# Rebuilding float64 weights in a borrowed PSUM buffer, with three smaller changes, in a fused RWKV-6 scan and feed-forward kernel

## The chip, the cores and the metric

The kernel runs on one core of one Trainium2 chip. The metric is device microseconds of one execution.

## The reference, cut to what matters

```python
# attention: r, k, v, w of (4, 8, 768, 48) in float32, u of (8, 48)
for t in range(S):
    cur = np.einsum('bhd,bhe->bhde', u[None] * kt, vt)
    y[:, :, t] = np.einsum('bhd,bhde->bhe', rt, state + cur)
    state = wt[:, :, :, None] * state + np.einsum('bhd,bhe->bhde', kt, vt)
# feed-forward on the 3072 tokens: x (3072, 384), w_in (384, 2048), w_out (2048, 384) in float64
h = x @ w_in
sp = np.maximum(h, 0.0) + np.log1p(np.exp(-np.abs(h)))
g = h * erf(sp)
out = (g @ w_out).astype(np.float32)
```

Two facts matter. The scan is serial in time, so it is done as a tree of levels. The weights arrive as float64 and the kernel works in float32, so it rebuilds each weight as a float32 from its two 32-bit words.

## The kernel before

There are twelve steps of 256 tokens (two batches of 128). A step of the scan has seven levels. Each level has small block products on TensorE (into `pp`; 64 in the trace's count, 32 in level 7, with two records in the trace for each matmul of the program), a multiplication by products of w on VectorE, and a masked copy. Then the output `y` is summed in PSUM, ScalarE evicts it, and the next step begins. Between these pieces, at eight "places" per step, TensorE gets dense work of earlier steps: input matmuls with `w_in` for the step before, output matmuls with `w_out` for the third step before. Steps 1 and 2 have input matmuls only, step 0 has none.

The weights come in 32 tiles, 16 of `w_in` and then 16 of `w_out`. `CONVERT` says how many are rebuilt at each place: 4 in step 0, 13 in step 1, 9 in step 2, 6 in step 3.

```python
        def scale(i):                       # three tiles ahead of join(i)
            ...
                base = wide.tile(list(low.shape), FP32, name="base")
                rest = wide.tile(list(low.shape), I32, name="rest")
                nc.scalar.mul(out=base[:], in_=high.bitcast(FP32), mul=2.0**-112)
                nc.scalar.mul(out=rest[:], in_=low.bitcast(U32), mul=2.0**-29)
        def join(i):
            ...
                bits = base[:].bitcast(I32)
                nc.vector.tensor_scalar(out=bits, in0=bits, scalar1=3, scalar2=None,
                                        op0=ALU.logical_shift_left)
                nc.vector.scalar_tensor_tensor(out=bits, in0=words[:, :, 1], scalar=-(1 << 31), in1=bits,
                                               op0=ALU.bitwise_and, op1=ALU.bitwise_or)
                nc.gpsimd.tensor_tensor(out=weights[i][0].bitcast(I32), in0=bits, in1=rest[:], op=ALU.add)
...
    def prepare(s):      # beside step s-1: R and K times u, and the products of w, on GpSimd
    ...
        for level in range(1, LOG + 1):     # in attend(s)
            ...                             # block products
            nc.vector.tensor_mul(halves, halves, view(tots[level - 1], ...))
            ...                             # masked copy, or ScalarE's copies into own and late
            aside(level)                    # CONVERT[s][level - 1] conversions
            fill()                          # the place's dense matmuls
        ...                                 # transposes, y matmuls, evictions of y, six small DMAs
        aside(LOG + 1)
        fill()
        ...                                 # state matmuls and the state's update
    CONVERT = ((0, 0, 0, 1, 0, 1, 1, 1), (1, 1, 1, 2, 2, 2, 2, 2), (1,) * 7 + (2,), (2, 2, 2))
```

## Time and profile before

| | before |
|---|---|
| time | 713.78 us median of 3 runs (708.8 to 714.29) |
| profiled execution | 709.5 us, granted TensorE clock 0.983 of full |
| TensorE busy / idle | 680.3 / 29.2 us |
| first block products of steps 1, 2, 3, 4 | 37.36, 81.66, 125.76, 187.6 us |

The time from one step's first block products to the next step's is that step's length. From step 4 on it is 54.83 us, all of it TensorE work, so everything at stake lies in the first 190 us. The prediction below shows these steps in a table and the waits that make them long.

The groups of instructions of the conversion (line, engine, operation, output and input, count; then busy us and mean ns of one; then the engine's idle time just before them and who ended it):

```profile
L153 DVE TENSOR_SCALAR base<-base 128x384 int32<-128x384 int32 x32 | 18.4, 576 | 1.0 <-ACT base L144 1.0
L156 DVE SCALAR_TENSOR_TENSOR base<-words,base 128x384 int32<-128x384 int32 x32 | 27.5, 858 | 1.1
```

VectorE idles for 1.0 us in all before its 32 shifts: the bases that ScalarE prepares three tiles ahead are nearly always there. A timeline gives start, duration, engine, line, operation; in brackets the idle time before it and who ended it.

```profile
71.55 1.01 POOL L160 TENSOR_TENSOR w_in_sb<-base,rest 128x384 int32<-128x384 int32 x1 [0.56 <-DVE base L156]
...
78.05 2.83 PE L372 MATMUL m<-xT,w_in_sb 128*128 128x256 f32 x12 [0.87 <-ACT h L379]
```

The first line is the 16th and last tile of `w_in`. In the program it belongs to the last place of step 1, behind the evictions of `y`. Yet it is done at 72.6 us, while the `y` matmuls still run (72.26 to 74.25), because its conversion needed nothing that comes before it in that place, and VectorE and GpSimd ran ahead. The group of matmuls that uses it starts at 78.05, 5.5 us later.

### The profile page before, as it was taken

How to read it: one execution, taken by the hardware profiler on the slowest of the kernel's cores; microseconds unless marked ns; L12 is line 12 of the kernel's file. 1: busy time of each engine (PE TensorE's matmuls, PEld its weight loads, DVE VectorE, ACT ScalarE, POOL GpSimd, SP SyncE). 2: the span in 40 equal slices, each digit the busy share in tenths (PEclk: the TensorE clock that was granted, in tenths of full speed). 3: DMA queues.
4: the chain of work that ended last, by engine and by line, in shares of the span. 5: the costliest groups of instructions: out<-in, count | busy, mean ns of one | idle time of the engine just before them, and what ended most of it. 6: DMA issues, size and time to landing. Idle time of an engine off the chain costs nothing.

```text
span 709.5 us, 18369 instructions
## 1 busy us (share of the span) xinstructions
PE 680.3 (96%) x8458; PEld 503.3 (71%) x8458; DVE 293.2 (41%) x282; ACT 309.5 (44%) x387; POOL 165.6 (23%) x161
## 2 busy tenths in 40 slices
PE   8788889979999999999999999999999999999998
PEld 6566767648768768867867867867866866868654
DVE  6789585842442442352352262262262342210200
ACT  2237848605605704713722722632631641642700
POOL 5758273440320330240150050050050000000000
PEclk9899999989999999999999999999999999999999
DMA  8465624200300300300300300300210000000000
GB/s 315 146 209 163 218 69 161 81 12 13 130 12 13 129 13 13 129 13 12 128 3 24 106 24 24 106 26 24 92 39 24 4 5 24 5 3 23 1 22 22
DMA packets 15837, 45.78 MB, mean 65 GB/s; under 512 B 2832, under 2 KB 7184, under 8 KB 14352
## 3 DMA queue, kind: packets, MB, share of 16 engines
q1 hardware_dynamic: 14608, 44.02, 18.7%
q8 instruction: 66, 1.08, 0.6%
q10 hardware_dynamic: 1152, 0.59, 0.3%
q14 instruction: 11, 0.09, 0.0%
HBM read 38.70 MB, written 4.72 MB: 61 GB/s over the span
## 4 chain that ended last, share of the span: by engine, by line
PE 81%; ACT 6%; DVE 4%; issue 4%; DMA 3%; POOL 2%; SPq 0%; ACTq 0%; POOLq 0%; DVEq 0%
PE m L401 35%; PE m L372 31%; PE pp L246 9%; PE y L309 3%; DMA in<-in_rkw 2%; DVE in L257 1%; PE y L301 1%; PE pp L335 1%; ACT sp L356 1%; PE pp L289 1%; DVE base L153 1%; ACT sp L385 1%; DVE own L266 1%; DMA mask_sb<-in_masks 1%; ACT rest L146 1%
## 5 line engine op out<-in xcount | busy, mean ns | idle before, releaser
L372 PE MATMUL m<-xT,w_in_sb 128*128 128x256 f32 x1152 | 267.0, 388 | 2.8 <-ACT h L379 2.7
L401 PE MATMUL m<-w_out_sb,h 128*128 128x384 f32 x768 | 259.5, 493 | 4.3 <-POOL w_out_sb L160 4.3
L372 PEld LDWEIGHTS m<-xT,w_in_sb 128*128 128x128 f32 x1152 | 218.0, 193 | 35.5 <-POOL w_in_sb L160 1.7
L401 PEld LDWEIGHTS m<-w_out_sb,h 128*128 128x128 f32 x768 | 143.2, 190 | 99.7 <-POOL w_out_sb L160 6.0
L257 DVE TENSOR_TENSOR in<-in,tot_sb 128x1024 f32<-128x1024 f32 x72 | 93.8, 1303 | 211.9 <-PE pp L246 209.7
L360 DVE TENSOR_TENSOR h<-h,sp 128x1024 f32<-128x1024 f32 x48 | 64.6, 1387 | 112.1 <-ACT sp L356 112.1
L410 ACT COPY o<-m 128x384 f32<-128x384 f32 x24 | 11.5, 479 | 220.4 <-PE m L401 220.4
L246 PEld LDWEIGHTS pp<-in 48*64 48x64 f32 (+1 forms) x4224 | 71.4, 132 | 50.9 <-issue 25.4
L379 ACT COPY h<-m 128x512 f32<-128x512 f32 x96 | 55.5, 582 | 93.1 <-PE m L372 92.8
L246 PE MATMUL pp<-in 48*64 48x64 f32 (+1 forms) x4224 | 81.3, 219 | 14.4 <-DVE in L257 11.6
L189 POOL TENSOR_TENSOR rk<-in,u_pair 128x1024 f32<-128x1024 f32 (+1 forms) x24 | 54.0, 2264 | 69.0 <-PE pp L246 58.9
L345 POOL TENSOR_TENSOR s<-s,tot_sb 128x384 f32<-128x384 f32 x8 | 6.7, 831 | 233.4 <-PE y L301 233.4
L205 POOL TENSOR_TENSOR tot_sb<-tot_sb 128x256 f32<-128x256 f32 (+2 forms) x72 | 50.8, 705 | 5.4
L356 ACT ACTIVATE sp<-sp 128x2048 f32<-128x2048 f32 x24 | 45.9, 1911 | 0.3
L385 ACT ACTIVATE sp<-h 128x2048 f32<-128x2048 f32 x24 | 45.9, 1911 | 0.3
L266 DVE COPY_PREDICATED own<-mask_sb,pp 128x512 f32<-128x512 int32 x48 | 40.7, 849 | 0.0
L144 ACT ACTIVATE base<-words 128x384 f32<-128x384 f32 x32 | 17.8, 556 | 41.5 <-POOL w_in_sb L160 18.1
L356 ACT ACT_TABLE_LOAD x24 | 30.8, 1283 | 0.4
L385 ACT ACT_TABLE_LOAD x24 | 30.8, 1283 | 0.4
L160 POOL TENSOR_TENSOR w_out_sb<-base,rest 128x384 int32<-128x384 int32 x16 | 18.5, 1158 | 43.2 <-DVE base L156 31.3
L156 DVE SCALAR_TENSOR_TENSOR base<-words,base 128x384 int32<-128x384 int32 x32 | 27.5, 858 | 1.1
L257 DVE TENSOR_TENSOR in<-in 128x1024 f32<-128x1024 f32 x12 | 27.4, 2283 | 0.3
(45 smaller groups left out, 331.6 us busy)
## 6 DMA issues: line engine op xcount, KB each, us to landing
in<-in_rkw SPq DMA_DIRECT2D x11, 1536.0 KB, 7.4
words<-in_moe_w_in SPq DMA_DIRECT2D x16, 384.0 KB, 4.3
words<-in_moe_w_out SPq DMA_DIRECT2D x16, 384.0 KB, 3.4
v<-in_v SPq DMA_DIRECT2D x12, 384.0 KB, 3.8
out<-o SPq DMA_DIRECT2D x24, 192.0 KB, 1.9
v<-in_v SPq DMA_DIRECT2D x12, 192.0 KB, 4.0
in<-in_rkw SPq DMA_DIRECT2D x2, 512.0 KB, 4.4
xT<-y SPq DMA_DIRECT2D x36, 16.0 KB, 3.9
```

What stands on the lines that cost most here:

```text
L156: nc.vector.scalar_tensor_tensor(out=bits, in0=words[:, :, 1], scalar=-(1 << 31), in1=bits, op0=ALU.bitwise_and, op1=ALU.bitwise_or,)
L189: engine.tensor_mul(rk1[:, x, n].rearrange("p n (t two) -> p n t two", two=2), in_t[:, x, n].rearrange("p n (t two) -> p n t two", two=2), ...
L205: nc.gpsimd.tensor_mul(new, pair[:, :, 0], pair[:, :, 1])
L246: nc.tensor.matmul(pp[s0 : s0 + m, e, n, :m], lhsT=rk[rows(e), 1, n, s0 : s0 + m], rhs=rk[rows(e), 0, n, t0 : t0 + m], start=True, stop=True,)
L257: nc.vector.tensor_mul(halves, halves, view(tots[level - 1], 0, [[1, 2], [2, nb], [0, half]]))
L266: nc.vector.copy_predicated(rights(own[:], half), rights(mask_sb[:, level - 1 : level, :].to_broadcast([P, NH, HC]), half), rights(got, half),
L356: nc.scalar.activation(sp[:], sp[:], AF.Erf)
L360: nc.vector.tensor_mul(h[:, part], h[:, part], sp[:, part])
L372: nc.tensor.matmul(ps[:, ff, :], lhsT=w_in_sb[:, g * FG + f + ff, kk * P : (kk + 1) * P], rhs=xT[:, kk, :], start=kk == 0, stop=kk == KT - 1,)
L379: nc.scalar.copy(h[:, f : f + FT, :], ps[:])
L385: nc.scalar.activation(sp[:], h[:], AF.Softplus)
L401: nc.tensor.matmul(ps[j][:], lhsT=gs[g][:, f, j * C : (j + 1) * C], rhs=w_out_sb[:, g * FG + f, :], start=g + f == 0, stop=g == NG - 1 and ...
```

## The change

The intent is to take work and contention off VectorE and GpSimd in the early steps. It has four parts.

1. **Conversion in PSUM.** `base` is written into a half of `y`, the attention output's buffer in PSUM (the memory that this program's matmuls write; its other buffers lie in SBUF), so VectorE's shift and and/or read at most one operand from SBUF and should no longer contend with GpSimd. Since `y` is in use by the scan, the base can't be prepared ahead: `begin` issues it on ScalarE inside the level, `finish` joins it after.
2. **u on ScalarE.** R and K are loaded a second time (1 MB per step) and ScalarE multiplies them by u in 8 small activations, in place of two GpSimd multiplications.
3. **Products of w on VectorE** for steps 1 to 3 (prepared in steps 0 to 2). For every step they are also moved to one place: all seven stand in level 3, where the kernel before has two in level 4 and five in level 5.
4. **The first step by halves**: its multiplications one batch at a time, with shorter filler matmuls.

```diff
-                base = wide.tile(list(low.shape), FP32, name="base")      # in scale(), three ahead
-                nc.scalar.mul(out=base[:], in_=high.bitcast(FP32), mul=2.0**-112)
+        def begin(i):                                                     # in the level itself
+                base = y[:, i % NE].rearrange("p j q t -> p (j q t)")[:, : high.shape[1]]
+                nc.scalar.mul(out=base, in_=high.bitcast(FP32), mul=2.0**-112)
+        def finish(i):
+                bits = wide.tile(list(rest.shape), I32, name="bits")
                 nc.vector.tensor_scalar(out=base, in0=base, ... logical_shift_left)
                 nc.vector.scalar_tensor_tensor(out=bits[:], in0=words[:, :, 1], ..., in1=base, ...)
@@ prepare
+        if s:
+            nc.sync.dma_start(out=rk1[:], in_=rkw[s][:, 0:2])
...
+        engine = nc.vector if 0 < s <= len(CONVERT) - 1 else nc.gpsimd
-            nc.gpsimd.tensor_mul(new, pair[:, :, 0], pair[:, :, 1])
+            engine.tensor_mul(new, pair[:, :, 0], pair[:, :, 1])
...
+                nc.scalar.mul(out=part, in_=part, mul=u_sb[:, p : p + 1])
@@ attend
+            aside(level)                    # begin: after the block products
...
+            parts = 1 if s else NJ          # step 0 by halves
             aside(level)                    # finish: where the conversion was
...
-        aside(LOG + 1)
+        for _ in range(2):
+            aside(LOG + 1)
         fill()
```

More of the change, by code (lines that the diff above doesn't have):

```diff
@@ L91 @@
     u_sb = const.tile([P, NP], FP32, name="u_sb")
-    u_pair = const.tile([P, 2, JP, 2], FP32, name="u_pair")
+    u_pair = const.tile([P, 2, NP, 2], FP32, name="u_pair")
     ident = const.tile([P, P], FP32, name="ident")
@@ L100 @@
     y = ps_y.tile([P, NE, NJ, NP // 2, C], FP32, name="y")
+    CONVERT = ((0, 0, 0, 1, 0, 1, 1, 1), (1, 1, 1, 2, 2, 2, 2, 2), (1,) * 7 + (2,), (2, 2, 2))
     loaded = {}
@@ L134, in load, with round_off @@
             held[i] = [words]
-        def scale(i):
+        def round_off(i):
             if i in held:
-                words = held[i][0]
-                low, high = words[:, :, 0], words[:, :, 1]
-                base = wide.tile(list(low.shape), FP32, name="base")
+                low = held[i][0][:, :, 0]
                 rest = wide.tile(list(low.shape), I32, name="rest")
-                nc.scalar.mul(out=base[:], in_=high.bitcast(FP32), mul=2.0**-112)
                 nc.scalar.mul(out=rest[:], in_=low.bitcast(U32), mul=2.0**-29)
-                held[i] += [base, rest]
-        def join(i):
+                held[i].append(rest)
+        def begin(i):
             if i in held:
-                words, base, rest = held.pop(i)
-                bits = base[:].bitcast(I32)
+                high = held[i][0][:, :, 1]
+                base = y[:, i % NE].rearrange("p j q t -> p (j q t)")[:, : high.shape[1]]
+                nc.scalar.mul(out=base, in_=high.bitcast(FP32), mul=2.0**-112)
+                held[i].append(base.bitcast(I32))
+        def finish(i):
+            if i in held:
+                words, rest, base = held.pop(i)
+                bits = wide.tile(list(rest.shape), I32, name="bits")
                 nc.vector.tensor_scalar(
-                    out=bits, in0=bits, scalar1=3, scalar2=None, op0=ALU.logical_shift_left
+                    out=base, in0=base, scalar1=3, scalar2=None, op0=ALU.logical_shift_left
                 )
                 nc.vector.scalar_tensor_tensor(
-                    out=bits, in0=words[:, :, 1], scalar=-(1 << 31), in1=bits,
+                    out=bits[:], in0=words[:, :, 1], scalar=-(1 << 31), in1=base,
                     op0=ALU.bitwise_and, op1=ALU.bitwise_or,
@@ L160, in join @@
                 nc.gpsimd.tensor_tensor(
-                    out=weights[i][0].bitcast(I32), in0=bits, in1=rest[:], op=ALU.add
+                    out=weights[i][0].bitcast(I32), in0=bits[:], in1=rest[:], op=ALU.add
                 )
-        for i in range(-5, len(weights)):
-            for ahead, stage in ((5, load), (3, scale), (0, join)):
-                if 0 <= i + ahead < len(weights):
-                    stage(i + ahead)
-            if i >= -1:
-                yield
+        for i in range(5):
+            load(i)
+        for i in range(3):
+            round_off(i)
+        done = 0
+        while True:
+            count = yield
+            count = min(count or 0, len(weights) - done)
+            for i in range(done, done + count):
+                begin(i)
+            yield
+            for i in range(done, done + count):
+                finish(i)
+                for ahead, stage in ((5, load), (3, round_off)):
+                    if i + ahead < len(weights):
+                        stage(i + ahead)
+            done += count
     def rows(e, n=D):
@@ L184, in prepare @@
         rk1 = att.tile([P, 2, JP, C], FP32, name="rk1", bufs=1)
-        parts = 1 if s else NJ
-        for i in range(parts):
-            n = slice(i * JP // parts, (i + 1) * JP // parts)
-            for x, engine in ((1, nc.gpsimd), (0, nc.gpsimd if s else nc.vector)):
-                engine.tensor_mul(
-                    rk1[:, x, n].rearrange("p n (t two) -> p n t two", two=2),
-                    in_t[:, x, n].rearrange("p n (t two) -> p n t two", two=2),
-                    u_pair[:, x, n, None, :].to_broadcast([P, JP // parts, C // 2, 2]),
-                )
-                if parts == 1:
-                    yield
+        if s:
+            nc.sync.dma_start(out=rk1[:], in_=rkw[s][:, 0:2])
+        else:
+            for j in range(NJ):
+                n = slice(j * NP, (j + 1) * NP)
+                for x, engine in ((1, nc.gpsimd), (0, nc.vector)):
+                    engine.tensor_mul(
+                        rk1[:, x, n].rearrange("p n (t two) -> p n t two", two=2),
+                        in_t[:, x, n].rearrange("p n (t two) -> p n t two", two=2),
+                        u_pair[:, x, :, None, :].to_broadcast([P, NP, C // 2, 2]),
+                    )
+        yield
         tots, tot = [], in_t[:, 2].rearrange("p n t -> p (n t)")
@@ L204, in prepare @@
             pair = tot.rearrange("p (n two) -> p n two", two=2)
-            nc.gpsimd.tensor_mul(new, pair[:, :, 0], pair[:, :, 1])
+            engine.tensor_mul(new, pair[:, :, 0], pair[:, :, 1])
             tot = new
             used += nb
-            if level == 2:
-                yield
         ready[s] = rk1, tots, tot
         yield
+        for p in range(NP if s else 0):
+            for x in range(2):
+                part = rk1[:, x].rearrange("p (j n) (t two) -> p j n t two", j=NJ, two=2)
+                part = part[:, :, p, :, x]
+                nc.scalar.mul(out=part, in_=part, mul=u_sb[:, p : p + 1])
+            yield
     def attend(s, xT, fill, aside):
@@ L230, in keep_busy @@
         def keep_busy():
-            ps = ps_m.tile([P, NP * C], FP32, name="m")
+            ps = ps_m.tile([P, NP // 2 * C], FP32, name="m")
             nc.tensor.matmul(
-                ps[:], lhsT=ident[:], rhs=in_t[:, 2, :NP], start=True, stop=True
+                ps[:], lhsT=ident[:], rhs=in_t[:, 2, : NP // 2], start=True, stop=True
             )
         for level in range(1, LOG + 1):
-            half, nb = 1 << (level - 1), JP * C >> level
+            half = 1 << (level - 1)
             rk = rk1[:] if level == 1 else RK
@@ L254, in attend @@
                 keep_busy()
-            halves = view(RK, half, [[SLOT - half, 2], [2 * half, nb], [1, half]])
-            nc.vector.tensor_mul(
-                halves, halves, view(tots[level - 1], 0, [[1, 2], [2, nb], [0, half]])
-            )
+            aside(level)
+            parts = 1 if s else NJ
+            for j in range(parts):
+                nb = JP // parts * C >> level
+                halves = view(
+                    RK, half + j * NP * C, [[SLOT - half, 2], [2 * half, nb], [1, half]]
+                )
+                nc.vector.tensor_mul(
+                    halves, halves,
+                    view(tots[level - 1], 2 * j * nb, [[1, 2], [2, nb], [0, half]]),
+                )
             got = pp[:].rearrange("p e n t -> p (e n) t")
@@ L434, in beside @@
             next(kind[of])
-    CONVERT = ((0, 0, 0, 1, 0, 1, 1, 1), (1, 1, 1, 2, 2, 2, 2, 2), (1,) * 7 + (2,), (2, 2, 2))
     ALONE = {1: (0, 0, 1, 1, 1, 1, 2, 2), 2: (0, 1, 1, 1, 1, 1, 1, 2)}
@@ L445 @@
     load_step(0, NJ)
-    for j in range(NJ):
-        for x in range(2):
-            nc.gpsimd.tensor_copy(out=u_pair[:, x, j * NP : (j + 1) * NP, x], in_=u_sb[:])
+    for x in range(2):
+        nc.gpsimd.tensor_copy(out=u_pair[:, x, :, x], in_=u_sb[:])
     for t in v0_bufs:
@@ L472, in aside @@
             def aside(level):
-                for _ in range(CONVERT[s][level - 1] if s < len(CONVERT) and level <= len(CONVERT[s]) else 0):
-                    next(conversion, None)
+                counts = CONVERT[s] if s < len(CONVERT) else ()
+                conversion.send(counts[level - 1] if level <= len(counts) else 0)
             attend(s, xTs[s], lambda: beside(s, next(places)), aside)
```

## The prediction

> **What bounds the kernel now.** I first read the page's busy rows and its 40 slices.
>
> ```profile
> PE 680.3 (96%) x8458; PEld 503.3 (71%) x8458; DVE 293.2 (41%) x282; ACT 309.5 (44%) x387; POOL 165.6 (23%) x161
> ...
> PE   8788889979999999999999999999999999999998
> ...
> DVE  6789585842442442352352262262262342210200
> ```
>
> TensorE is busy 96% of 709.5 us. Its gaps lie in the first nine slices (some 160 us) and the last. A cut at the first block product of each step of the scan, with the engines' busy times, says how much each stage is above the floor:
>
> ```profile
> 0.00:37.36 37.36, 29.55 (x575) 21.44 (x575) 25.18 (x26) 12.32 (x22) 23.70 (x35) 0.91 0.70 232
> 37.36:81.66 44.30, 37.40 (x624) 29.95 (x621) 36.67 (x42) 26.13 (x44) 26.26 (x22) 0.96 0.64 201
> 81.66:125.76 44.10, 37.64 (x652) 31.36 (x648) 31.37 (x36) 32.04 (x47) 20.97 (x19) 0.92 0.40 121
> 125.76:187.67 61.91, 57.61 (x720) 42.02 (x720) 30.04 (x30) 27.39 (x37) 15.32 (x16) 0.94 0.17 58
> 187.67:242.50 54.83, 54.83 (x716) 40.93 (x719) 20.89 (x18) 23.41 (x28) 11.46 (x10) 1.00 0.14 50
> ```
>
> The columns after the length are PE, PEld, DVE, ACT, POOL, granted clock, DMA share, GB/s. Step 4 is wholly TensorE: 54.83 us, as are steps 5 and on; nothing in this change makes it shorter. Step 3 has the same TensorE work plus 7.1 us. For steps 1 and 2 I take the scan (54.83 - 21.5 for eight groups of output matmuls of 2.68 us - 21.5 for eight of input matmuls of 2.69 us = 11.8 us) plus 21.5 us of input matmuls, 33.3 us, and in step 1 some 2 us of filler: they are 9 and 11 us above that. Step 0 has no dense work to hide its waits. All that the change can win is in these waits, some 27 us of 709 in steps 1 to 3 and a few in step 0. Who waits for whom says what they are:
>
> ```profile
> PE pp L246 <- DVE in L257: 11.6, 13, 3.5
> PE m L401 <- POOL w_out_sb L160: 4.3, 1, 4.3
> PE pp L246 <- issue: 2.8, 3, 1.4
> PE m L372 <- ACT h L379: 2.7, 3, 1.6
> ```
>
> A level of the scan runs VectorE's multiplication (L257) and then the next block products; in steps 1 and 2 VectorE is behind. Why, the timeline tells:
>
> ```profile
> 41.10 0.35 DVE L153 TENSOR_SCALAR base<-base 128x384 int32<-128x384 int32 x1
> ...
> 44.00 1.90 POOL L189 TENSOR_TENSOR rk<-in,u_pair 128x1024 f32<-128x1024 f32 x1
> 44.19 1.93 DVE L153 TENSOR_SCALAR base<-base 128x384 int32<-128x384 int32 x1
> ```
>
> The shift of the conversion takes 0.35 us alone and 1.93 us while GpSimd multiplies by u. Over the run it averages 0.576 us, the and/or (L156) 0.858 against 0.56 at best.
>
> **What the Trainium skill says.** "SBUF — State Buffer", Who interferes with whom: a VectorE instruction in a two-port mode shuts GpSimd out and the reverse, one with two SBUF inputs contends with GpSimd's reads, one with at most one SBUF input outside those modes does not. The lines above agree. "VectorE: DVE Perf Modes", Why PSUM operands drop a tier: a PSUM operand takes the fp32 two-port mode away. So a shift in PSUM no longer contends but is longer alone; VectorE's copy of 384 elements out of PSUM (L348) takes 0.555 us here, against 0.35. "ScalarE: Activation LUTs", What ACT_TABLE_LOAD costs: an ACTIVATE takes 186 ns + 0.833 ns per element, 93 ns more with a per-partition operand, and neighbours overlap by 93 ns: my estimate for 128 elements is 386 - 93, about 0.3 us each. For 384 elements it says 506 ns, L144 took 556. "TensorE: Matmul & The Clock Gate", Part 1: an idle window of about 3.4 us halves the clock until a busy one passes. The trace agrees: after TensorE was 55 to 63% busy from 20 to 28 us the granted clock was 0.50 from 28 to 32.
>
> **The change part by part.**
>
> Conversion in PSUM. 32 tiles. VectorE's pair was 0.576 + 0.858 = 1.43 us each; it becomes about 0.56 + 0.56 = 1.12, with no stretch from GpSimd: 32 x 0.31 = 10 us of VectorE time less over steps 0 to 3. But y is also where the attention output is summed, so the base can only be written when y is free, and ScalarE now writes it inside the level (it was three tiles ahead). The built instruction order shows two costs. (a) The conversion in the last place of steps 0 and 1 has its base behind the evictions of y and behind three DMA issues on ScalarE's queue (2.2 us in the trace), and VectorE has this conversion ahead of the state copy and of the next step's first multiplication. Before, that multiplication started 1.3 us after the first block products began (38.70 against 37.36). Now, from the end of y: evictions 1.2, issues 2.2, base 0.5, shift and and/or 1.1, state copies 1.1, multiplication 1.2: 7.4 us to the second block products, where it was 4.5 (35.55 to 40.07). Steps 1 and 2 have no dense matmuls in their first place, so TensorE waits: +3 us, twice. (b) The base of level 1 in steps 2 and 3 is queued behind a softplus, an erf and two table loads (6.4 us), and in step 2 the base of level 7 behind an erf; the y matmuls must wait for that conversion: +2 us.
>
> u by ScalarE. GpSimd loses two multiplications of 2.35 us in 11 steps (51 us), ScalarE gains 8 x 0.3 = 2.4 us a step. From step 4 all this lies beside TensorE: nothing. In steps 1 to 3 it removes the remaining stretches of VectorE (the 2.9 us multiplication and 4.55 us gate at 91 to 96 us are 1.2 and 2.4 alone) and lets GpSimd's adds go at once: about -2 us per step. The second load is 1 MB per step beside a queue that is a third idle after step 0; in step 0 it comes behind the first load of step 1.
>
> Products of w on VectorE for steps 1 to 3. Seven dependent multiplications of 512 down to 8: 0.69, 0.42, 0.29, 0.22, 0.19, 0.17, 0.16 by VectorE's 1.22 us for 1024 and 0.69 for 512, with the waits 2.5 us a step, three times: 7.5 us of VectorE time, which eats three quarters of the 10 us above. In step 0 they stand behind level 3 and wait for the load of step 1, which landed at 21.7 us (GpSimd's L189 waited for it until 21.73). VectorE would be there at 17: it now stalls until 21.7 and then works to 24.2, so the fourth multiplication starts 5.5 us later than the 18.75 us of before.
>
> First step by halves. A level was about 2.55 us (block products 1.16, multiplication 1.23, waits); with halves VectorE's own 0.69 + 0.69 + 0.70 for the masked copy, 2.1 us, sets it: -0.45 a level over three levels before the stall and about -0.5 for the four after it, where the old ones were also stretched to 2.24.
>
> Sum, by start of each step (positive is later): step 1 at +1.5 (stall +5.5, halves and stretches -4). Its second products at +5 (a: +3, a cold clock after the gap +0.5); its levels 2 to 7 are then VectorE-bound, 19 to 20 us against 21.6, and its end loses the 1.6 us wait and the 1.7 us of half clock of before: step 2 at +1.5. In step 2 +3 (a), -3 from the gate and multiplication at 91 to 97 and its half clock, +2 (b): step 3 at about +3. In step 3 the wait for the last output weights (4.3 us, then half clock) is a fixed point: the and/or that feeds them ends at about 148 us before; the chain now loses some 3 us of stretches and has start +3. So step 4 starts within a microsecond or two of before. The remaining 520 us are the same TensorE work. Net -1 us with an uncertainty of some 5.
>
> **Rivals.** One: the author's intent wins; VectorE's relief counts fully, the new waits for ScalarE overlap with waits that exist anyway, and no half clock occurs: up to -12 us, 700. For it: VectorE is 83% busy in step 1 and the 1.93 us stretches are on the path. Against: the dependency through ScalarE's in-order queue and 7.5 us of new work. Two: the waits add up; the extra megabyte delays step 1's load, TensorE goes cold in each gap: +8 us, 721. For it: DMA share is about 1.0 until 20 us, and the gap before level 4 is longer than a clock window. Against: the slack before the w_out wait absorbs part. Three: ScalarE becomes the bound of step 2 (32 us busy of 44, +2.4): not by itself, but its order delays the gate; this is in (b).
>
> **Range and chances.** Before is 713.78 (708.8 to 714.29, so the runs of one kernel already differ by 5). With -1 from the working and a little trust in the intent I say 711, range 702 to 721. Over 2% faster needs 699.5, about half of all waits gone: 0.08. Over 2% slower needs 728: 0.05.
>
> **What would show it.** Right: shift and and/or near 0.56 us each and steady; VectorE waiting for the load of step 1 at 17 to 22 us before the products of w; TensorE idle 3 to 5 us before the second block products of steps 1 and 2, with VectorE waiting for ScalarE's base; steps from 4 on at 54.8 us. Wrong: step 4 starting over 6 us earlier or later than 187.7, a shift in PSUM over 0.8 us, or ScalarE's scaling of R and K on TensorE's path.

## The result, and the profile after

The kernel after takes 734.28 us (median of 4 runs, 732.27 to 734.89); the kernel before, in the same rounds, 713.06 (4 runs, 708.8 to 714.29). Executions over 1.5% slower than the fastest of the same kernel are left out of the means. Ratios here are the mean time of one kernel's fast runs over that of the other's of the same rounds, so they differ a little from the ratio of the medians quoted. This one is 1.0303, with a 95% interval of 1.0263 to 1.0344. It is slower by 3%, well above the predicted range.

The busy row and the slices of TensorE and VectorE from the page of the kernel after:

```profile
PE 689.1 (94%) x8458; PEld 512.7 (70%) x8458; DVE 272.6 (37%) x310; ACT 338.7 (46%) x475; POOL 93.3 (13%) x116
...
PE   7769678797999999999999999999999999999998
...
DVE  6758277373233243243243243143143143210100
```

The intent was met in full: VectorE is busy 20.6 us less than before (293.2), GpSimd 72.3 us less (165.6), ScalarE 29.2 us more (309.5). TensorE, which sets the time, is idle 733.1 - 689.1 = 44.0 us instead of 29.2, and busy 8.8 us longer with the same 8458 matmul records, which fits its lower granted clock (0.955 of full on average, 0.983 before). Together 23.6 us, the difference of the two profiled spans (733.1 and 709.5).

The windows cut at each step's first block products, with the columns of the prediction's table:

```profile
0.00:39.73 39.73, 32.13 (x574) 25.95 (x574) 24.99 (x38) 12.84 (x26) 11.48 (x23) 0.66 0.72 245
39.73:96.59 56.86, 41.46 (x624) 33.87 (x620) 34.03 (x51) 33.96 (x61) 19.95 (x14) 0.82 0.56 179
96.59:145.07 48.48, 37.74 (x650) 31.33 (x648) 30.77 (x42) 31.16 (x48) 13.48 (x8) 0.93 0.40 127
145.07:211.11 66.04, 59.59 (x720) 43.01 (x720) 27.36 (x32) 32.14 (x48) 16.48 (x18) 0.92 0.21 70
211.11:265.94 54.83, 54.83 (x716) 40.92 (x719) 18.67 (x18) 25.82 (x36) 4.89 (x9) 1.00 0.20 69
```

Step 1 grew from 44.30 to 56.86 us, steps 2 and 3 by about 4 each, step 0 by 2.4. Step 4 is unchanged. TensorE's waits (engine, awaited instruction's tile and line; total us, times, longest):

```profile
PE pp L272 <- DVE in L289: 16.6, 10, 6.2
PE m L435 <- POOL w_out_sb L169: 5.7, 2, 5.3
PE m L406 <- POOL w_in_sb L169: 4.8, 1, 4.8
PE y L334 <- DVE bits L165: 4.2, 1, 4.2
PE y L342 <- DVE bits L165: 2.9, 1, 2.9
```

The wait for VectorE's multiplication was 11.6 us before and is 16.6; the wait for `w_out` was 4.3 and is 5.7. Three waits are new, 11.9 us together. Each of them is for a conversion (L162 is the shift, L165 the and/or, L169 GpSimd's add). The groups of the conversion say why:

```profile
L162 DVE TENSOR_SCALAR y<-y 128x384 int32<-128x384 int32 x32 | 18.4, 574 | 44.8 <-ACT y L155 44.5
L165 DVE SCALAR_TENSOR_TENSOR bits<-words,y 128x384 int32<-128x384 int32 x32 | 17.7, 554 | 2.9 <-issue 0.5
```

The pair now takes 0.574 + 0.554 = 1.13 us where it took 1.43, and it no longer stretches. But VectorE idles 44.8 us before its 32 shifts, where it idled 1.0, nearly all of it for ScalarE's base (L155). The timeline at the start of step 1:

```profile
39.73 1.16 PE L272 MATMUL pp<-rk 48*64 48x64 f32 x64
...
40.37 3.19 ACTq L356 DMA_DIRECT2D xT<-y  x3
...
43.60 0.51 ACT L155 ACTIVATE y<-words 128x384 f32<-128x384 f32 x1 [3.27 <-issue]
...
44.14 0.57 DVE L162 TENSOR_SCALAR y<-y 128x384 int32<-128x384 int32 x1 [8.50 <-ACT y L155]
...
46.35 1.23 DVE L289 TENSOR_TENSOR in<-in 128x1024 f32<-128x1024 f32 x1
...
47.72 1.56 PE L272 MATMUL pp<-in 48*64 48x64 f32 x48 [6.20 <-DVE in L289]
```

This conversion belongs to the last place of step 0. Its base stands behind the evictions of `y` and three DMA issues in ScalarE's order, its shift stands ahead of step 1's first multiplication in VectorE's order, and TensorE has no dense work there. From first to second block products it takes 7.99 us; before, 2.71 (37.36 to 40.07), where the same line was:

```profile
40.07 1.16 PE L246 MATMUL pp<-in 48*64 48x64 f32 x64 [0.49 <-DVE in L257]
```

The same view at the end of step 1, after the change:

```profile
80.04 1.95 PE L342 MATMUL y<-own,v 128*48 128x64 f32 x32 [2.88 <-DVE bits L165]
...
86.69 2.06 ACTq L356 DMA_DIRECT2D xT<-y  x3
...
88.79 1.05 ACT L155 ACTIVATE y<-words 128x384 f32<-128x384 f32 x2 [2.14 <-issue]
...
91.23 1.00 POOL L169 TENSOR_TENSOR w_in_sb<-bits,rest 128x384 int32<-128x384 int32 x1 [10.10 <-DVE bits L165]
...
92.28 2.93 PE L406 MATMUL m<-xT,w_in_sb 128*128 128x256 f32 x6 [4.75 <-POOL w_in_sb L169]
```

Here is the 16th tile of `w_in` again. It was ready at 72.6 us before; now its base stands on ScalarE behind an erf (until 84.17 us), the copies that evict `y` and three DMA issues, so the tile is ready at 92.23 us, and the last six input matmuls wait 4.75 us for it. They then run at half clock (2.93 us for six records, against 2.83 for twelve before). TensorE also waited at the first line shown, 2.88 us, because the level-7 conversions held `y`.

So the 23.6 us can be placed. Each figure is a difference of two start times read from the timelines of the two profiled executions:

| stretch | before | after | change |
|---|---|---|---|
| start to first block products of step 1 | 37.36 | 39.73 | +2.4 |
| step 1, first to second block products | 2.71 | 7.99 | +5.3 |
| step 1, from there to the first `y` matmuls | 32.19 | 32.32 | +0.1 |
| step 1, from there to step 2 | 9.40 | 16.55 | +7.2 |
| step 2, up to the transposes ahead of `y` | 32.22 | 32.53 | +0.3 |
| step 2, from there to step 3 | 11.88 | 15.95 | +4.1 |
| step 3, up to the output matmuls that waited for `w_out` | 22.43 | 24.89 | +2.5 |
| all the rest | 561.3 | 563.1 | +1.8 |

### The profile page after: what moved, and what is told of

Its sections match the earlier page's. It is cut to its first block, busy times and chain, and to the rows that moved or that the text cites. A ratio compares the mean times of both kernels' runs of the same rounds, so it can differ in the third digit from the quotient of the medians.

```text
span 733.1 us, 18465 instructions
## 1 busy us (share of the span) xinstructions
PE 689.1 (94%) x8458; PEld 512.7 (70%) x8458; DVE 272.6 (37%) x310; ACT 338.7 (46%) x475; POOL 93.3 (13%) x116
## 4 chain that ended last, share of the span: by engine, by line
PE 76%; ACT 4%; POOL 1%; DVE 1%; issue 1%; ACTq 0%; DVEq 0%; POOLq 0%
PE m L435 33%; PE m L406 28%; PE pp L272 9%; PE y L342 3%; PE y L334 2%; PE pp L322 1%; PE pp L369 1%; POOL tot_sb L226 1%; ACT sp L419 1%; ACT sp L390 1%; ACT L390 1%; ACT L419 1%; POOL w_out_sb L169 1%; DVE y L162 0%; DVE bits L165 0%
## 5 line engine op out<-in xcount | busy, mean ns | idle before, releaser
L289 DVE TENSOR_TENSOR in<-in,tot_sb 128x1024 f32<-128x1024 f32 (+1 forms) x78 | 91.1, 1173 | 218.5 <-PE pp L272 216.5
L272 PEld LDWEIGHTS pp<-in 48*64 48x64 f32 (+1 forms) x4224 | 75.7, 140 | 52.4 <-issue 34.4
L272 PE MATMUL pp<-in 48*64 48x64 f32 (+1 forms) x4224 | 85.6, 228 | 18.0 <-DVE in L289 16.6
L394 DVE TENSOR_TENSOR h<-h,sp 128x1024 f32<-128x1024 f32 x48 | 60.5, 1301 | 108.1 <-ACT sp L390 108.1
L413 ACT COPY h<-m 128x512 f32<-128x512 f32 x96 | 55.4, 579 | 84.9 <-PE m L406 84.8
L236 ACT ACTIVATE rk<-rk,u_sb 128x128 f32<-128x128 f32 x88 | 31.3, 405 | 11.3 <-DMA rk<-in_rkw 10.9
L162 DVE TENSOR_SCALAR y<-y 128x384 int32<-128x384 int32 x32 | 18.4, 574 | 44.8 <-ACT y L155 44.5
L169 POOL TENSOR_TENSOR w_out_sb<-bits,rest 128x384 int32<-128x384 int32 x16 | 24.7, 1544 | 47.9 <-DVE bits L165 47.9
L146 ACT ACTIVATE rest<-words 128x384 int32<-128x384 uint32 x32 | 17.6, 550 | 27.0 <-DMA words<-in_moe_w_in 11.0
L169 POOL TENSOR_TENSOR w_in_sb<-bits,rest 128x384 int32<-128x384 int32 x16 | 21.7, 1359 | 56.7 <-DVE bits L165 55.0
L155 ACT ACTIVATE y<-words 128x384 f32<-128x384 f32 x32 | 16.6, 520 | 21.6 <-DVE bits L165 13.8
```

Source lines behind the costliest of these rows:

```text
L236: nc.scalar.mul(out=part, in_=part, mul=u_sb[:, p : p + 1])
L272: nc.tensor.matmul(pp[s0 : s0 + m, e, n, :m], lhsT=rk[rows(e), 1, n, s0 : s0 + m], rhs=rk[rows(e), 0, n, t0 : t0 + m], start=True, stop=True,)
L289: nc.vector.tensor_mul(halves, halves, view(tots[level - 1], 2 * j * nb, [[1, 2], [2, nb], [0, half]]),)
L394: nc.vector.tensor_mul(h[:, part], h[:, part], sp[:, part])
L413: nc.scalar.copy(h[:, f : f + FT, :], ps[:])
```

## The experiments

Each was run with a profile and three timed rounds beside the kernel before; all gave the right result. The first question was which part costs the time, and whether shorter filler and the early half clock (0.50 from 12 to 36 us after, 1.00 until 24 before) were a rival cause.

**a_words_sbuf**: the kernel after, with the conversion of before.

```diff
-                base = y[:, i % NE].rearrange("p j q t -> p (j q t)")[:, : high.shape[1]]   # begin(i)
+                base = wide.tile(list(low.shape), FP32, name="base")                        # scale(i), three ahead
```

> The changed kernel with the conversion of before (words in SBUF, scaled three tiles ahead of the join), the other three parts kept. Theory T: the 21 us lost come from the conversion, whose base now waits for y to be free and for ScalarE's queue, so with the old conversion the time is 704 to 716 us. Rival R1: the halved filler and halved multiplications of the first step let TensorE's clock go to half from 12 us on and the loss follows from that: 725 us or more. Rival R2: the scaling by u on ScalarE and the second load delay things: 725 us or more.

711.3 us (708.08 to 712.47) against 712.48: ratio 0.998 (0.9941 to 1.002). All of the loss is gone, and with it the waits for `w_in` and for `bits`.

**b_psum_only**: the kernel before, with the conversion of after and nothing else.

```diff
-                base = wide.tile(list(low.shape), FP32, name="base")                        # scale(i), three ahead
+                base = y[:, i % NE].rearrange("p j q t -> p (j q t)")[:, : high.shape[1]]   # begin(i)
```

> The kernel before with only the conversion of the change (base in y's PSUM, written inside the level). T: 727 to 737 us, and TensorE waits for VectorE's and/or before y and for GpSimd's w_in words, as in the changed kernel. R1 and R2: within 5 us of before (708 to 718).

730.41 us, ratio 1.0262 (1.0224 to 1.0299). Put in alone, this part brings 2.6 of the 3.0%, and the three new waits with it (4.6 us for `w_in`, 4.8 and 3.6 ahead of the `y` matmuls).

**c_base_sbuf_late**: the kernel after, with the base in an SBUF buffer of its own but still written inside the level. This parts two things that the change joins: that the base must wait for `y` (and `y` for the base), and that it is late in ScalarE's order.

```diff
-                base = y[:, i % NE].rearrange("p j q t -> p (j q t)")[:, : high.shape[1]]
+                base = wide.tile(list(high.shape), FP32, name="base")                       # still in begin(i)
```

> The changed kernel with the base in an SBUF buffer of its own, but still written inside the level by ScalarE. It separates y's lifetime from ScalarE's order. If only the tie to y counts, it is as fast as the run with the conversion of before (within 4 us). If only the late place in ScalarE's queue counts, it stays within 3 us of the changed kernel (731 to 737). I expect between: the 2.9 and 4.2 us before y go, the waits behind the DMA issues and the softplus stay: 723 to 729 us.

724.94 us, ratio 1.0182 (1.014 to 1.0224), halfway. TensorE's waits in its profile:

```profile
PE pp L272 <- DVE in L289: 14.6, 9, 5.0
PE m L435 <- POOL w_out_sb L169: 6.0, 1, 6.0
PE m L406 <- POOL w_in_sb L169: 5.1, 1, 5.1
```

The waits of the `y` matmuls for `bits` are gone; the wait for `w_in` and the one at the start of step 1 (4.98 us) stay. So the late place in ScalarE's order is by itself enough for these two. By the ratios, the tie to `y` costs (1.0303 - 1.0182) x 712.5 = 8.6 us and the late place in ScalarE's order (1.0182 - 0.998) x 712.5 = 14.4 us, each uncertain by some 4 us by their intervals. That the base lies in SBUF does not blur this: VectorE's pair took 0.41 + 0.72 = 1.13 us in c, as much as in the kernel after.

**d_full_filler**: the kernel after, with filler matmuls of 512 columns as before.

```diff
-            ps = ps_m.tile([P, NP // 2 * C], FP32, name="m")
+            ps = ps_m.tile([P, NP * C], FP32, name="m")
```

> The changed kernel with the filler matmul of the first step at its old width of 512. R1: the clock stays full until 20 us at least as before, and the time falls by over 8 us, below 726. T: the clock may recover in the first step but the time stays at 729 to 735, since later waits are for the conversion.

732.99 us, ratio 1.0291 (1.0261 to 1.0321). The granted clock was 1.00 until 24 us in this profile and 0.50 from 12 us in that of the kernel after; step 1 begins at 39.24 and 39.73 us. So the early half clock is not what costs the time, and the rival falls. The rival was right on one point: of the fast profiles, seven of the nine with the shorter filler were at 0.50 by 16 us (not a and i), and none of the seven with the longer one.

The second group puts in the other parts alone.

**e_u_only**: the kernel before, with u on ScalarE.

```diff
-            for x, engine in ((1, nc.gpsimd), (0, nc.gpsimd if s else nc.vector)):
+        if s:
+            nc.sync.dma_start(out=rk1[:], in_=rkw[s][:, 0:2])     # and 8 nc.scalar.mul by u_sb
```

> The kernel before with only the second load of R and K and u applied by ScalarE; the products of w stay on GpSimd. My prediction counted -2 us in each of steps 1 to 3 from the stretches that GpSimd's two multiplications cause on VectorE: 706 to 711 us. If ScalarE's extra 2.8 us a step or the extra megabyte is on the path: 716 us or more.

708.03 us against 712.37, ratio 0.9951 (0.9923 to 0.9979), a gain of 3.5 us. By steps, step 1 went from 44.3 to 41.4 and step 3 from 61.8 to 58.6, but step 2 from 44.1 to 47.9: ScalarE is busy 35.8 us of it (32.0 before), and the `y` matmuls wait 2.7 us for ScalarE's copy into `late`. This run also shows how little was left for PSUM to save: with u off GpSimd, VectorE's pair takes 0.44 + 0.78 = 1.22 us in SBUF, against 1.43 before and 1.13 in the kernel after. Two thirds of the gain that the borrowed buffer was meant for come without it.

**f_w_only**: the kernel before, with the products of w for steps 1 to 3 on VectorE.

```diff
-            nc.gpsimd.tensor_mul(new, pair[:, :, 0], pair[:, :, 1])
+            engine.tensor_mul(new, pair[:, :, 0], pair[:, :, 1])  # VectorE for s = 1, 2, 3
```

> The kernel before with only the products of w for steps 1 to 3 on VectorE. The prediction said 7.5 us more of VectorE work and a stall on the load of step 1 until 21.7 us, by itself a loss: 715 to 722 us, with VectorE idle before the products in step 0. If it is neutral (the work fits in gaps): 710 to 714.

713.98 us, ratio 1.0039 (1.0011 to 1.0066), a loss of 2.8 us. That is less than the 715 to 722 expected, and inside the range given for no effect, though the interval leaves out 1. The run is not quite part 3 of the change: it leaves the products in levels 4 and 5, where VectorE waits 0.32 us for the load of step 1, against 2.03 us in level 3 of the kernel after.

**g_halves_only**: the kernel before, with step 0 by halves and the shorter filler.

```diff
-            halves = view(RK, half, [[SLOT - half, 2], [2 * half, nb], [1, half]])
+            for j in range(parts):                                # two halves in step 0
```

> The kernel before with only the halved multiplications of step 0 and the halved filler matmul. Prediction: -1 to -3 us (709 to 712). If the shorter filler lets the clock drop early and that carries on: 716 or more.

711.99 us (710.0 to 717.48), ratio 1.0019 (0.9969 to 1.007): no effect that these runs resolve. In the profiled run, the slowest of the four, step 0 was 40.26 us long, 2.9 more than before, with the clock at 0.50 from 12 us.

The four parts alone (part 3 at its old places) add up to 2.62 - 0.49 + 0.39 + 0.19 = 2.7%, close to the whole, 3.0%.

**i_no_w_step0**: kernel a, with the products of w for step 1 back on GpSimd, so that VectorE need not wait for the second load in step 0.

```diff
-        engine = nc.vector if 0 < s <= len(CONVERT) - 1 else nc.gpsimd
+        engine = nc.vector if 1 < s <= len(CONVERT) - 1 else nc.gpsimd
```

> The run with the old conversion (711.3) with the products of w for step 1 given back to GpSimd, those for steps 2 and 3 left on VectorE. If the stall of VectorE on the load of step 1 in step 0 (5.4 us of TensorE's idle time, then half clock) is on the path: 705 to 708 us. If the lost time is hidden later: 710 to 712.

708.15 us, ratio 0.9936 (0.9902 to 0.9969) against 0.998 (0.9941 to 1.002) for a. The intervals overlap, so a gain is not shown by the times alone. In the profile of a, as in the kernel after, VectorE stood until 21.4 us for the load of step 1 before it could multiply, and TensorE waited 5.4 us; in i that wait is gone (one of 3.42 us, for nothing that the profile shows, stands near it) and step 0 is 36.51 us long against 38.72. That points to the stall; how much of part 3's loss it is stays open.

The third group leaves the conversion in PSUM and changes only its places, that is `CONVERT`.

**k_places**: none in level 7 and none in the last place of any step; the last four in levels 1 and 2 of step 3. (The four runs of this group replace the same line; it is shown removed only here.)

```diff
-    CONVERT = ((0, 0, 0, 1, 0, 1, 1, 1), (1, 1, 1, 2, 2, 2, 2, 2), (1,) * 7 + (2,), (2, 2, 2))
+    CONVERT = ((0, 0, 0, 2, 2, 2, 0, 0), (2, 2, 2, 2, 2, 2, 0, 0), (2, 2, 2, 2, 1, 1, 0, 0), (2, 2, 0))
```

> The changed kernel, words in PSUM as they are, with only the counts of conversions per place altered so that none falls in level 7 or in the last place of steps 0 to 2, where y is written and evicted (step 0: 2,2,2 in levels 4 to 6; step 1: 2 in levels 1 to 6; step 2: 2,2,2,2,1,1; step 3: 2,2). T in its narrow form (the places where y and ScalarE's long instructions collide with the conversion, not PSUM itself): the waits before y (2.9 and 4.2) and for the w_in words (4.8) and the late first multiplication of step 1 go, 712 to 720 us. If words in PSUM are slow wherever they stand: 728 or more.

719.98 us, ratio 1.0125 (1.0093 to 1.0156). Step 1 is 44.8 us, as before the change. The waits for `bits`, `w_in` and `w_out` are all gone from its list of waits; by far the largest left is:

```profile
PE pp L272 <- DVE in L289: 25.7, 16, 6.0
```

The conversions now delay VectorE's multiplications inside the levels instead (16.6 us in the kernel after): step 0 is 3.6 us longer than after, step 2 is 4.0 longer. One caution: k has 28 conversions done before step 3, not 26, and none in its level 3. That removes the `w_out` wait (step 3 is 54.8 us), so part of its gain is not due to level 7 and the last place.

**l_no_first**: as k, and none in level 1 of steps 2 and 3, where the base stands behind a softplus and an erf.

```diff
+    CONVERT = ((0, 0, 0, 2, 2, 2, 0, 0), (2, 2, 2, 2, 2, 2, 0, 0), (0, 2, 2, 2, 2, 2, 0, 0), (0, 2, 2))
```

> As the run with the counts moved out of level 7 and the last place, and in addition no conversion in level 1 of steps 2 and 3, where its base stands behind a softplus and an erf on ScalarE (VectorE idle 5.2 us there in step 2). T: 2 to 5 us less than that run's 719.98, so 715 to 718. If that wait lies beside others: 719 to 721.

722.08 us (median of all four; 721.56 of its three fast runs), ratio 1.0118 (1.0086 to 1.015) of the fast runs, above the 715 to 718 expected; one run was slow (741.1) and its profile fell in that run, so there are no steps to read. No gain over k was shown: it moved two conversions back into level 3 of step 3, and the run doesn't separate that from what it avoided.

**o_no_last**: the last place alone is emptied.

```diff
+    CONVERT = ((0, 0, 0, 1, 1, 1, 1, 0), (1, 1, 2, 2, 2, 2, 2, 0), (2, 2, 1, 1, 1, 1, 2, 0), (2, 2, 2))
```

> The changed kernel with no conversion in the last place of steps 0 to 2, those moved to earlier places (level 7 keeps its conversions). If the last place is most of the loss (late first multiplication of step 1: 5 us; wait for w_in words 4.8 us and half clock): 720 to 726 us, with level 7's waits before y still there. If it is the smaller part: 729 or more.

728.35 us, ratio 1.0219 (1.0195 to 1.0242): less than expected. Step 1 did what it should. It falls from 56.9 to 47.6 us, its second block products come 2.7 us after its first, and the wait for `w_in` is gone. But step 2 rises from 48.5 to 55.4. I had put two conversions into its level 7, and there one line of its waits took the gain back:

```profile
PE y L334 <- DVE bits L165: 6.0, 1, 6.0
```

**p_no_seventh**: level 7 alone is emptied.

```diff
+    CONVERT = ((0, 0, 0, 1, 1, 1, 0, 1), (1, 2, 2, 2, 2, 2, 0, 2), (1, 1, 1, 1, 2, 1, 0, 2), (2, 2, 2))
```

> The changed kernel with no conversion in level 7 of steps 0 to 2, those moved to earlier levels (the last place keeps its own). If level 7's waits before y (2.9 and 4.2 us) count in full: 725 to 729 us. If the wait for the w_in words in the last place swallows them: 731 or more.

728.25 us, ratio 1.0224 (1.0208 to 1.0241). Step 2 falls from 48.5 to 44.9 us: its wait of 4.2 us is gone. Step 1 stays at 56.2: the `y` matmuls no longer wait, but the input matmuls behind them wait 6.0 us for `w_in` instead of 4.8, and the second block products still come late. Level 7's wait in step 1 was hidden behind the last place's.

The last group looks for a version that beats both kernels.

**m_u_earlier**: the kernel before, with u on ScalarE and four conversions of step 3 moved into step 2.

```diff
-    CONVERT = (..., (1,) * 7 + (2,), (2, 2, 2))
+    CONVERT = (..., (1, 1, 1, 2, 2, 2, 2, 2), (1, 1))
```

> A candidate for a better version: the kernel before with u by ScalarE, and four of step 3's six conversions moved into levels 4 to 7 of step 2 (1,1,1,2,2,2,2,2 there, then 1,1), so that the last output weights are there in time. TensorE's wait of 3.2 us for them in the run with u alone goes: 703 to 706 us; if VectorE in step 2 becomes the bound instead: 708 or more.

703.43 us against 712.93, ratio 0.9868 (0.9835 to 0.9901). The `w_out` wait of step 3 is gone (54.8 us); step 2 has 4.1 us of waiting for ScalarE's `late`.

**n_u_earlier_late**: as m, with that copy of step 2 on VectorE.

```diff
-                nc.scalar.copy(late[:HC], got[:HC])
+                (nc.vector.tensor_copy if s == 2 else nc.scalar.copy)(late[:HC], got[:HC])
```

> As the candidate with u and earlier conversions, and step 2's copy of the last level out of PSUM by VectorE, which does not stand behind an erf: the wait of 2.7 us before the second half of y and the half clock after it (7.61 us for matmuls of 5.38) go too: 699 to 703 us; if VectorE delays the copy as much: no gain over that candidate.

703.24 us, ratio 0.9858 (0.983 to 0.9886), the best of all, though not resolved from m. Its windows of steps 1, 2 and 3:

```profile
37.11:78.50 41.39, 35.68 (x624) 28.56 (x620) 34.59 (x42) 28.60 (x52) 22.03 (x20) 1.00 0.73 235
78.50:122.30 43.80, 36.24 (x652) 29.96 (x648) 36.30 (x45) 35.47 (x58) 23.16 (x21) 0.96 0.53 160
122.30:178.18 55.88, 54.88 (x716) 40.94 (x713) 21.64 (x22) 27.92 (x40) 9.23 (x12) 1.00 0.20 69
```

The copy gave 2.2 us in step 2 (46.0 in m), and step 3 lost half of that: its output matmuls now wait 1.0 us for ScalarE.

**q_all_but_words**: n's two moves on top of i (which has the halves, the shorter filler, u on ScalarE, and the products of w for steps 2 and 3 on VectorE).

```diff
-    CONVERT = (..., (1,) * 7 + (2,), (2, 2, 2))
+    CONVERT = (..., (1, 1, 1, 2, 2, 2, 2, 2), (1, 1))
-                nc.scalar.copy(late[:HC], got[:HC])
+                (nc.vector.tensor_copy if s == 2 else nc.scalar.copy)(late[:HC], got[:HC])
```

> The better version (u by ScalarE, earlier conversions in SBUF, VectorE's copy in step 2) with the halves of step 0, the short filler and the products of w for steps 2 and 3 on VectorE added. If those parts add nothing once GpSimd is relieved of u: 702 to 706 us; if they help: below 701.

703.79 us, ratio 0.9883 (0.9862 to 0.9905): with u on ScalarE kept, the other parts of the change add nothing.

## Why the prediction was wrong

The forecast of 711 us and its range failed; 0.05 had been given to what happened. Part of its working held, some terms were mis-sized, and two steps failed.

**Held.** The pair came to 1.13 us against an estimate of 1.12, and steady (shifts of 0.55 to 0.67 us, where those before ranged up to 1.93), which agrees with what the prediction took from the skill on PSUM operands and on contention. VectorE's stall on the load of step 1 was there (until 21.29 us). Step 1 began at +2.4 against a forecast of +1.5, partly by luck: VectorE reached the products at 19.26 us, not 17, because the levels before ran at half clock, so it stalled 2.0 us, and the halves that were to pay for the stall brought nothing alone (g). Later steps are at 54.83 us.

**Read too strongly, or added up wrongly.** The prediction set the half clock from 28 to 32 us beside an idle window and called it agreement, but TensorE had been 55 to 63% busy, not idle. The clear case is in a: TensorE idle for 5.40 us up to 25.13, and the clock at 0.50 from 24 us. In its sum, step 2 at +1.5 does not follow from its own terms: +5, then 19.5 us instead of 21.6, then 3.3 us of waits gone, make -0.4.

**Mis-sized: term (a) at the start of step 1.** The mechanism was as described, but from the end of `y` to the second block products it took 8.6 us (39.09 to 47.72), not 7.4. Against the 4.5 before that is +4.1, not +3. (Counted from the first block products, as in the table above, it is +5.3, because those began 0.64 us after the end of `y` instead of 1.81.) Three DMA issues on ScalarE took 3.19 us here, where the 2.2 of the trace before had been used.

**Mis-sized: term (b).** The level-7 base of step 2 stood behind an erf, as said (it starts at 132.61 us, the erf at 130.80). It cost TensorE 4.2 us rather than 2, plus half clock for the `y` matmuls after it (1.96 us for 32 against 1.09 before). The level-7 conversions of step 1 do the same, 2.9 us, and were not in the sum. The base at level 1 of step 3, also named in (b), comes up under the second failed step.

**Mis-sized: the halves.** Three levels at -0.45 and four at -0.5 were to bring 3.4 us; alone (g) they changed the time by +0.2%, with an interval on both sides of zero.

**Failed: "+3 us, twice".** The prediction looked at the last-place conversion of step 1 only through VectorE's next multiplication, and there step 2 lost nothing: its second block products come 2.58 us after its first, before and after. What it missed is a reader of the result. The counts add up to 4 + 13 = 17 conversions by the end of step 1, so the 16th tile, the last of `w_in`, is rebuilt in that last place, and the input matmuls of the same place need it. Before, VectorE and GpSimd were done with it 5.5 us before those matmuls began; the new place in ScalarE's order took that freedom away (c, which has no tie to `y`, keeps a wait of 5.1 us). From the first `y` matmuls to step 2, step 1 lost 7.2 us. Runs k and o, without last-place conversions, show step 1 at 44.8 and 47.6 us; p, which keeps them, at 56.2. The gain that the prediction expected towards the end of step 1 (a 1.6 us wait and 1.7 us of half clock gone) lies before the `y` matmuls; it came for the most part (a 0.57 us wait and full clock after it) and was used up by the wait at level 7.

**Failed: step 3's wait "is a fixed point".** It was read as a fixed time on the clock (148 us), held there by a start 3 us later and 3 us of stretches saved. The first line is of the kernel before, the other three of the kernel after:

```profile
148.19 3.19 PE L401 MATMUL m<-w_out_sb,h 128*128 128x384 f32 x4 [4.30 <-POOL w_out_sb L160]
...
151.84 1.91 ACT L390 ACTIVATE sp<-sp 128x2048 f32<-128x2048 f32 x1
153.66 1.05 ACT L155 ACTIVATE y<-words 128x384 f32<-128x384 f32 x2
...
169.96 2.93 PE L435 MATMUL m<-w_out_sb,h 128*128 128x384 f32 x4 [5.32 <-POOL w_out_sb L169]
```

The last four tiles of `w_out` are rebuilt in levels 2 and 3 of step 3, so the wait travels with the step. It ended 22.43 us after the step began before, 24.89 after, and so absorbed none of the delay of steps 0 to 2 and added 2.5 us. The trace shows where the delay began: in level 1 the bases stood behind an erf until 153.66 us, and VectorE's multiplication of level 2 started 11.9 us after the step's start, 7.7 before (157.00 and 133.44 us). Where the last conversions were moved out of level 3 (k, m), step 3 fell to 54.8 us. So step 2, forecast at +1.5, began at +14.9 (96.59 against 81.66), and step 3, which was to swallow what delay there was, added to it.

**The rivals.** The second one, waits adding up, was the right family, but its 721 us was still short by 13, and its cause (the extra megabyte) was not it: u on ScalarE, with the same second load, gains 3.5 us alone, and the load of step 1 was not later (VectorE used it from 21.29 us, GpSimd from 21.73 before). The third, ScalarE as the bound of step 2, shows in e: of the -2 us per step forecast for u, steps 1 and 3 gave 2.9 and 3.2, and step 2 gave 3.8 back. The relief of VectorE inside the levels was real and small: in step 1, second block products to the `y` matmuls, it offset the new level-7 wait of 2.9 us almost exactly (+0.1).

What stays open: how much of k's gain over the kernel after is due to level 7 and the last place and how much to the four early `w_out` tiles, and why l gained nothing. The early half clock differed between executions with the same first step (0.50 from 12 us in the kernel after; in a only from 24 us). It goes with the shorter filler in seven of nine profiles, but what decides it was not pursued, since d shows that it hardly moves the time.

## What to carry to other kernels

Before moving a producer into a borrowed buffer, count not only what each instruction costs but how far ahead its engine used to run, and list every reader of the result: work that was free because it was done 5.5 us before its reader becomes critical when it is tied to another engine's order. A wait that ends at a certain time in one trace is not fixed in time; find the instruction it hangs on and ask what moves that. Here VectorE lost 20.6 us of busy time and the kernel got 21 us slower, while moving work earlier (four tiles) and off one contended engine (u) gained 1.3% (m).

## What the Trainium skill lacked or had wrong

- "DMA: Bandwidth & Descriptors", section "Issuing engines are not separate DMA queues", calls the sequencer's time to initiate a DMA usually small relative to the DMA. One of the 16 KB copies here took ScalarE 0.60 us to issue (median) and 3.8 us to land, so the sentence holds for one. But three in a row took 3.19 and 2.06 us at the two ends of step 1 and held ScalarE's next instruction back for 3.27 and 2.14 us, in the chain that TensorE waited for. The section does not say that a compute engine's own work waits for its issues, and gives no figure.
- "ScalarE: Activation LUTs", section "What ACT_TABLE_LOAD costs": estimated from its figures, an activation of 128 elements with a per-partition operand takes 386 ns, and two in a row 0.68 us with the 93 ns overlap. The 88 activations by u took 405 ns on average, and two in a row 0.70 to 0.72 us: a little more, up to 6%.
- No page that I read says that a buffer borrowed between two of its uses ties the engines' orders together. By the ratios it cost 8.6 us here (after against c; uncertain by some 4 us), of a loss of 21.
